# Sorted-block attention and a four-expert layer on one core: the key mix in full-width matmuls, a new order of batch 1's stages, and four smaller edits

## The chip, the cores and the metric

The kernel runs on one core of a Trainium2 chip. The metric is the time of one execution on the device, in microseconds (us). Medians are quoted with their range. A ratio is the mean time of one kernel's fast runs over the mean time of the other kernel's fast runs of the same rounds, so it is not quite the ratio of the medians that stand beside it; its 95% interval is given. The profile shows one execution: for the kernel before a further one of 374.80 us. Its span is some 1.8 us shorter than its time.

Engines are called TensorE (PE in the profile, its weight loads PEld), VectorE (DVE), ScalarE (ACT), GpSimd (POOL) and the sync engine (SP), which only issues transfers.

## The reference, cut to what matters

```python
# q, k, v: (4 batches, 8 heads, 768, 64); 8 blocks of 96 rows; sort_net: (4, 8, 8, 8)
for _ in range(5):                        # Sinkhorn rounds: a soft permutation P of the blocks
    P = exp(P - max(P)); P /= P.sum(-1); P /= P.sum(-2)
k_sorted = einsum('bhij,bhjcd->bhicd', P, k_blocks)     # "mix" of keys; the same for v
attn = softmax(q_blocks @ k_sorted_blocks.T / 8)        # within each block
x = (attn @ v_sorted_blocks)  -> (3072, 512)
# four experts, each x -> 1024 -> 512, weighted by domain_probs
out = sum_e p[:, e] * (relu(x @ w1[e]) @ w2[e])
```

## The kernel before

Batches go through in order. While the experts work on batch b, the attention of batch b+1 is slipped between their matmuls: a plan names, for every slot (after each group of first-layer matmuls and after each of seven second-layer products), the stages to issue. A stage is one of: mix of values (`st_v`), mix of keys (`st_k`), transpose of queries by a transfer (`st_q`), scores (`st_s`), outputs (`st_a`), transpose of outputs by a transfer (`st_x`), or loads. Two heads form a "pair"; a batch has four, and three pairs of row blocks ("row block pair" c = 0, 1, 2) in the expert part.

```python
def st_k(b, pr):                          # 12 matmuls, 64 weight columns each
    ps = psa([P, R, P], F32, ...)         # psa: pool of two buffers; psm: another pool of two
    for r in range(R):                    # R = 6 rows of a partition
        for hh in range(2):
            nc.tensor.matmul(ps[ds(D * hh, D), r, :], head(b, "k", h)[:, r, :], PIk..., ...)
    nc.scalar.copy(kT..., ps...)          # one copy of 128 x 768

PLAN0 = [ ...                             # batch 1, slots of c = 1 and 2, cut
    (1, 0, st_q, 1), (1, 0, st_s, 0), (1, 0, st_n, 2), (1, 1, st_k, 1), (1, 1, st_v, 2), (1, 2, st_v, 3),
    (1, 3, st_a, 0), (1, 4, st_x, 0), (1, 3, st_q, 2), (1, 4, st_n, 3), (1, 5, st_s, 1), (1, 6, st_k, 2),
    (1, 8, st_a, 1), ..., (1, 10, st_s, 2), ..., (1, 11, st_k, 3), (1, 12, st_a, 2), ...,
    (2, 1, st_x, 2), ..., (2, 2, st_s, 3), (2, 8, st_a, 3), (2, 9, st_x, 3) ]

def chunk(b, c, slot, done=()):
    chunk_first(...)                      # first layer; VectorE evacuates each group
    for w in range(1, 4 if b or c else 3):
        h_sums(E - 1, w)                  # sums that the products p5, p6, p7 need
    ...                                   # then products p1, p4, p2, p5, p6, p7, p3
            next(sums0)                   # weight differences for the next batch, on VectorE
            tt(u2[:], product("p6", ...), p1[:], ALU.add)

def store(n, tile):
    nc.sync.dma_start(o[:, 2 * c + n, :], tile[:])
```

The softmax here doesn't subtract the row's maximum and nothing guards it: scores larger than these inputs give would overflow.

## Time and profile before

375.43 us median of 3 runs (375.1 to 376.16).

| part of the page | value |
|---|---|
| span | 373.0 us |
| TensorE busy | 366.3 us, 98% |
| VectorE, ScalarE, GpSimd busy | 261.2, 73.9, 87.9 us |
| chain that ended last | TensorE 87%, transfers 8% |

The chain is followed back from the last instruction, at each step to what released it. The groups of instructions give busy time and mean nanoseconds after the first bar, and idle time ahead of them after the second. Two groups of the kernel before, the key mix and its copy:

```profile
L376 PE MATMUL ps_k<-PIk,nat_k 128*64 128x128 f16 x144 | 6.3, 223 | 0.0
...
L383 ACT CAST kT<-ps_k 128x768 f16<-128x768 f32 x12 | 9.6, 799 | 35.4 <-PE ps_k L376 35.3
```

"128*64" is the array that the weights fill: half of the columns. The mix itself is 6.3 of 366 us.

### The profile page before, as it was taken

Reading aid. Unit: us, or ns where it says so; the run is one execution under the profiler, and the core shown is the slowest. Engines: PE = TensorE matmul, PEld = TensorE weight load, DVE = VectorE, ACT = ScalarE, POOL = GpSimd, SP = SyncE. Lnnn points to the kernel's source line nnn. Section 1 sums busy time; section 2 is a strip of 40 time slices with the busy share of each in tenths; the row PEclk is TensorE's granted clock in tenths of the full one; section 3 lists DMA queues with packets and bytes.
Section 4 is the critical chain, followed back from the end, with each engine's and each line's share of the span. In section 5 each row is a group of like instructions: output and inputs, shape, how many; then the busy total and the mean of one; then the engine's idle time right before and its main releaser. Section 6 shows DMA issues by size and latency. Waiting matters only on the chain.

```text
span 373.0 us, 9188 instructions
## 1 busy us (share of the span) xinstructions
PE 366.3 (98%) x4013; PEld 314.9 (84%) x4013; DVE 261.2 (70%) x470; ACT 73.9 (20%) x120; POOL 87.9 (24%) x122
## 2 busy tenths in 40 slices
PE   8999999999999999999999999999999999999996
PEld 8785858888888888888898888888889888888885
DVE  5654798679888774795694684696695693774872
ACT  2673330423210233012100224012101000000000
POOL 8772101804577203002911000000000001001001
PEclk9999999999999999999999999999999999999999
DMA  7999999999995658642962322505203101121001
GB/s 104 207 207 229 208 209 197 190 163 143 187 154 137 110 77 133 126 80 43 124 71 48 101 66 60 138 2 77 79 2 79 57 15 44 56 47 50 19 3 56
DMA packets 69603, 38.25 MB, mean 103 GB/s; under 512 B 40374, under 2 KB 64444, under 8 KB 69564
## 3 DMA queue, kind: packets, MB, share of 16 engines
q0 software_dynamic: 34640, 17.83, 37.6%
q1 hardware_dynamic: 34924, 19.85, 26.0%
q8 instruction: 31, 0.51, 0.6%
q14 instruction: 8, 0.07, 0.1%
HBM read 42.00 MB, written 6.34 MB: 130 GB/s over the span
## 4 chain that ended last, share of the span: by engine, by line
PE 87%; DMA 8%; DVE 2%; POOL 1%; issue 1%; ACT 0%; DVEq 0%
PE ps_h L730 40%; PE ps_p L763 35%; DMA w<-in_moe_w_dram 4%; PE ps_o L670 3%; DMA qT<-natq 2%; PE ps_w L241 2%; DMA natq<-in_q_dram 2%; PE ps_h L635 1%; PE ps_s L393 1%; PE ps_a L425 1%; PE ps_k L376 1%; PE ps_v L345 1%; POOL sn L284 0%; DVE xsl L410 0%; POOL T L136 0%
## 5 line engine op out<-in xcount | busy, mean ns | idle before, releaser
L730 PE MATMUL ps_h<-xT,w 128*128 128x256 f16 x1440 | 163.0, 273 | 0.0
L730 PEld LDWEIGHTS <-w 128*128 128x128 f16 x1440 | 139.5, 98 | 17.8
L736 DVE SCALAR_TENSOR_TENSOR Hb<-ps_h,pb 128x1024 f16<-128x1024 f32 x90 | 110.1, 1224 | 40.1 <-PE ps_h L730 38.3
L763 PEld LDWEIGHTS <-Sb 128*128 128x128 f16 x720 | 69.5, 98 | 9.6 <-issue 0.5
L763 PEld LDWEIGHTS <-Hb 128*128 128x128 f16 x540 | 52.1, 98 | 6.8 <-issue 0.4
L790 POOL TENSOR_TENSOR oa<-u,p 128x256 f32<-128x256 f32 x9 | 6.5, 723 | 176.7 <-issue 161.9
L763 PE MATMUL ps_p<-w,Sb 128*128 128x256 f16 x360 | 43.2, 273 | 0.3 <-DVE u L863 0.3
L763 PE MATMUL ps_p<-w,Hb 128*128 128x256 f16 x360 | 43.2, 273 | 0.0
L763 PE MATMUL ps_p<-T,Sb 128*128 128x256 f16 x360 | 42.3, 273 | 0.0
L400 ACT ACTIVATE ET<-ps_s 96x768 f16<-96x768 f32 x24 | 18.1, 802 | 54.4 <-PE ps_s L393 54.4
L114 POOL DMA_DIRECT2D natq<-in_q_dram x24 | 19.9, 851 | 14.3 <-DMA w<-in_moe_w_dram 10.2
L778 ACT COPY p<-ps_p 128x256 f32<-128x256 f32 x9 | 3.4, 373 | 93.3 <-PE ps_p L763 50.1
L763 PE MATMUL ps_p<-T,Hb 128*128 128x256 f16 x180 | 21.6, 273 | 0.0
L715 DVE TENSOR_TENSOR Sb<-Sb,Hb 128x512 f16<-128x512 f16 x45 | 19.6, 436 | 0.4
L717 DVE TENSOR_TENSOR Sb<-Hb 128x512 f16<-128x512 f16 x45 | 18.8, 418 | 0.0
L713 DVE TENSOR_TENSOR Sb<-Hb 128x512 f16<-128x512 f16 x45 | 18.8, 417 | 0.0
L410 DVE TENSOR_TENSOR xsl<-ps_a,rz 96x512 f16<-96x512 f32 x24 | 16.5, 686 | 0.8
L719 DVE TENSOR_TENSOR Sb<-Hb,Sb 128x512 f16<-128x512 f16 x45 | 16.6, 427 | 0.0
L383 ACT CAST kT<-ps_k 128x768 f16<-128x768 f32 x12 | 9.6, 799 | 35.4 <-PE ps_k L376 35.3
L788 DVE TENSOR_TENSOR u<-ps_p,p 128x256 f32<-128x256 f32 x9 | 3.8, 426 | 17.9 <-PE ps_p L763 17.9
L351 ACT CAST vo<-ps_v 128x768 f16<-128x768 f32 x12 | 9.5, 801 | 21.5 <-PE ps_v L345 19.8
L103 POOL DMA_DIRECT2D nat_k<-in_k_dram x8 | 6.1, 767 | 31.9 <-PE ps_k L376 27.8
(131 smaller groups left out, 300.9 us busy)
## 6 DMA issues: line engine op xcount, KB each, us to landing
w<-in_moe_w_dram POOLq DMA_DIRECT2D x7, 1024.0 KB, 27.1
pb<-p_dram SPq DMA_DIRECT2D x12, 512.0 KB, 5.1
nat_k<-in_k_dram POOLq DMA_DIRECT2D x8, 384.0 KB, 7.4
nat_v<-in_v_dram POOLq DMA_DIRECT2D x8, 384.0 KB, 8.6
vs<-vo SPq DMA_DIRECT2D x36, 66.0 KB, 4.6
natq<-in_q_dram POOLq DMA_DIRECT2D x24, 96.0 KB, 4.5
out_dram<-ob SPq DMA_DIRECT2D x9, 256.0 KB, 2.3
out_dram<-oa SPq DMA_DIRECT2D x9, 256.0 KB, 2.3
```

Source lines behind the costliest of these rows:

```text
L114: nc.gpsimd.dma_start(t[:, h // 2, :, h % 2, :], q[b, h].rearrange("(t p) d -> p t d", p=P))
L383: nc.scalar.copy(kT[:, 0:S].rearrange("p (i r c) -> p i r c", i=NB, r=R), ps.rearrange("p r (i c) -> p i r c", c=CP),)
L400: nc.scalar.activation(ETs[2 * (pr % 2) + hh][:, 0:S].rearrange("c (a x) -> c a x", a=2), pss[hh][0:BLK, :, 0:HS], AF.Exp, bias=0.0, scale ...
L410: nc.vector.tensor_tensor(xsl[:, :, hh, :].rearrange("c (a i) d -> c a i d", a=2), av[:, :, :, 0:D], rz[:].broadcast_to([BLK, 2, HB, D]), ...
L670: nc.tensor.matmul(ps, h0(fc)[:, ds(t * P, P)], w2sb[0][:, fc, :], start=(fc == 0), stop=(fc == NFC - 1),)
L713: tt(sm[0], blk(0, 1), blk(1, 1), ALU.add)
L715: tt(sm[1], sm[0], blk(0, 0), ALU.subtract)
L717: tt(sm[2], blk(0, 0), blk(0, 1), ALU.subtract)
L719: tt(sm[3], blk(1, 0), sm[1], ALU.subtract)
L730: nc.tensor.matmul(ps[:, f, :], w1sb[e][:, kc, ds((4 * g + f) * P, P)], xT[:, kc, ds(2 * c * P, 2 * P)], start=(kc == 0), stop=(kc == NKC ...
L736: nc.vector.scalar_tensor_tensor(out=Hb[:, e, ds(4 * g, 4), :], in0=ps[:], scalar=0.0, op0=ALU.max, in1=pb[:, ds(e, 1), :].broadcast_to([P ...
L763: nc.tensor.matmul(ps[:], lhs(e, f), Ts[e][rhs][:, f, :], start=(e == es[0] and f == 0), stop=(e == E - 1 and f == KH - 1),)
```

## The change

It has six parts: **keys** (two rows at a time, full-width weights, hence four copies of a quarter each), **plan** (batch 1's outputs later, but for the last pair's; its second scores and its last outputs one slot sooner), **sums** (the last sums and the weight differences later on VectorE, the first product in the other pool), **start** (query transposes in the fifth Sinkhorn round), **copy** (one copy from VectorE to ScalarE) and **store** (the last row block in two parts).

```diff
 def warm(n):
-        ps = psA.tile(...)
+        ps = psM.tile(...)
 for it in range(5):
-        if it >= 3:
-            h_q(it - 3, 0, nc.scalar.copy)
-            warm(20 - 8 * (it - 3))
+        if it == 4:
+            for qd in range(2):
+                h_q(qd, 0, nc.scalar.copy)
+            warm(30)
 def st_k(b, pr):
-        ps = psa([P, R, P], F32, ...)
-        for r in range(R):
-            for hh in range(2):
-                nc.tensor.matmul(ps[ds(D * hh, D), r, :], head(b, "k", h)[:, r, :], PIk..., ...)
-        nc.scalar.copy(kT..., ps...)
+        ps = psa([P, 2, 512], F32, ...)
+        for hh in range(2):
+            for a in range(R // 2):
+                nc.tensor.matmul(pk[:, hh, a, :],
+                    head(b, "k", h)[:, ds(2 * a, 2), :].rearrange("p r d -> p (r d)"), PIk..., ...)
+        for hh in range(2):
+            for r in range(2):
+                nc.scalar.copy(kT[ds(D * hh, D), r], pk[ds(D * r, D), hh]...)
 PLAN0 (slots of c = 1 and 2, cut)
-        (1, 3, st_a, 0), (1, 4, st_x, 0), (1, 5, st_s, 1), (1, 6, st_k, 2), (1, 8, st_a, 1),
-        (1, 10, st_s, 2), (1, 11, st_k, 3), (1, 12, st_a, 2), (2, 2, st_s, 3), (2, 8, st_a, 3), (2, 9, st_x, 3),
+        (1, 4, st_s, 1), (1, 5, st_a, 0), (1, 6, st_x, 0), (1, 7, st_k, 2), (1, 9, st_a, 1),
+        (1, 11, st_s, 2), (2, 0, st_a, 2), (2, 1, st_k, 3), (2, 3, st_s, 3), (2, 7, st_a, 3), (2, 8, st_x, 3),
 chunk
-        for w in range(1, 4 if b or c else 3):
+        for w in range(1, 4 if b else 2 if c else 3):
             h_sums(E - 1, w)
+            parts = 2 if (b, c) == (B - 1, R // 2 - 1) else 1
+            if parts == 2:
+                nc.sync.dma_start(o[:, 2 * c, 0:DH], oa1)      # right after p2
 ...                                                            # and oa2 alone at the end
-            nc.scalar.copy(p1[:], product("p1", ..., "b11"))
+            nc.scalar.copy(p1[:], product("p1", ..., "b11", psm if c == 1 else psa))
+            if c == 1: h_sums(E - 1, 2); h_sums(E - 1, 3)      # after p4
             f2()
+            if c == 2: h_sums(E - 1, 2); h_sums(E - 1, 3)      # after p2
-            next(sums0)
             tt(u2[:], product("p6", ...), p1[:], ALU.add)
+            next(sums0)                                        # the second one likewise after u3
-        [(h_w, 1, vec), (h_a, 0, 2)],
+        [(h_w, 1, act), (h_a, 0, 2)],
```

More of the change, by code (lines that the diff above doesn't have):

```diff
@@ L237, in warm @@
     def warm(n):
-        ps = psA.tile([P, 4, P], F32, tag="ps", name=f"ps_w_{state['n']}")
+        ps = psM.tile([P, 4, P], F32, tag="ps", name=f"ps_w_{state['n']}")
         state["n"] += 1
@@ L371, in st_k @@
     def st_k(b, pr):
-        ps = psa([P, R, P], F32, f"ps_k_{b}_{pr}")
-        for r in range(R):
-            for hh in range(2):
-                h = 2 * pr + hh
+        ps = psa([P, 2, 512], F32, f"ps_k_{b}_{pr}")
+        pk = ps[:, :, 0:R // 2 * P].rearrange("p h (a x) -> p h a x", x=P)
+        for hh in range(2):
+            h = 2 * pr + hh
+            for a in range(R // 2):
                 nc.tensor.matmul(
-                    ps[ds(D * hh, D), r, :],
-                    head(b, "k", h)[:, r, :],
+                    pk[:, hh, a, :],
+                    head(b, "k", h)[:, ds(2 * a, 2), :].rearrange("p r d -> p (r d)"),
                     PIk[(b * H + h) // 4][:, h % 4, :, :].rearrange("p i c -> p (i c)"),
@@ L381, in st_k @@
                 )
-        kT = kTs[pr % 2]
-        nc.scalar.copy(
-            kT[:, 0:S].rearrange("p (i r c) -> p i r c", i=NB, r=R),
-            ps.rearrange("p r (i c) -> p i r c", c=CP),
-        )
+        kT = kTs[pr % 2][:, 0:S].rearrange("p (i a r c) -> p r a i c", a=R // 2, r=2, c=CP)
+        for hh in range(2):
+            for r in range(2):
+                nc.scalar.copy(
+                    kT[ds(D * hh, D), r],
+                    pk[ds(D * r, D), hh].rearrange("p a (i c) -> p a i c", c=CP),
+                )
     def st_s(b, pr):
@@ L601 @@
         (0, 9, st_v, 0), (0, 10, st_q, 0), (0, 10, st_v, 1), (0, 11, st_k, 0), (0, 11, st_n, 1), (1, 0, st_q, 1),
-        (1, 0, st_s, 0), (1, 0, st_n, 2), (1, 1, st_k, 1), (1, 1, st_v, 2), (1, 2, st_v, 3), (1, 3, st_a, 0),
-        (1, 4, st_x, 0), (1, 3, st_q, 2), (1, 4, st_n, 3), (1, 5, st_s, 1), (1, 6, st_k, 2), (1, 8, st_a, 1),
-        (1, 7, st_lv, 0), (1, 9, st_x, 1), (1, 10, st_s, 2), (1, 9, st_lv, 1), (1, 9, st_q, 3), (1, 11, st_k, 3),
-        (1, 12, st_a, 2), (1, 12, st_lk, 0),
-        (2, 0, st_lq, 0), (2, 1, st_x, 2), (2, 2, st_lk, 1), (2, 2, st_s, 3), (2, 8, st_a, 3), (2, 9, st_x, 3),
+        (1, 0, st_s, 0), (1, 0, st_n, 2), (1, 1, st_k, 1), (1, 1, st_v, 2), (1, 2, st_v, 3), (1, 3, st_q, 2),
+        (1, 4, st_s, 1), (1, 4, st_n, 3), (1, 5, st_a, 0), (1, 6, st_x, 0), (1, 7, st_k, 2), (1, 7, st_lv, 0),
+        (1, 9, st_a, 1), (1, 9, st_q, 3), (1, 9, st_lv, 1), (1, 10, st_x, 1), (1, 11, st_s, 2), (1, 12, st_lk, 0),
+        (2, 0, st_a, 2), (2, 0, st_lq, 0), (2, 1, st_k, 3), (2, 2, st_x, 2), (2, 2, st_lk, 1), (2, 3, st_s, 3),
+        (2, 7, st_a, 3), (2, 8, st_x, 3),
     ]
@@ L757, in chunk, with product @@
         sm = lambda n: (lambda e, f: Sb[:, n, e, ds(f * P, P)])
-        def product(n, lhs, rhs):
-            ps = psm([P, DH], F32, f"ps_{n}_{b}_{c}")
+        def product(n, lhs, rhs, pool=psm):
+            ps = pool([P, DH], F32, f"ps_{n}_{b}_{c}")
             for e in es:
@@ L797, in chunk @@
             slot()
-            nc.sync.dma_start(o[:, 2 * c, :], oa[:])
+            if parts == 2:
+                nc.sync.dma_start(o[:, 2 * c, DH:Dm], oa2)
+            else:
+                nc.sync.dma_start(o[:, 2 * c, :], oa[:])
             return
         def f1():
-            nc.scalar.copy(p1[:], product("p1", blk(0, 0), "b11"))
+            nc.scalar.copy(p1[:], product("p1", blk(0, 0), "b11", psm if c == 1 else psa))
             slot()
@@ L857, in chunk @@
             f4()
-            f2()
+            if c == 1:
+                h_sums(E - 1, 2)
+                h_sums(E - 1, 3)
+            f2()
+            if c == 2:
+                h_sums(E - 1, 2)
+                h_sums(E - 1, 3)
             f5()
@@ L861, in chunk @@
                 h_sums(e, 4)
-            next(sums0)
             tt(u2[:], product("p6", sm(1), "t2"), p1[:], ALU.add)
             slot()
+            next(sums0)
             gtt(oa2, u2[:], oa2, ALU.add)
-            next(sums0)
             tt(u3[:], product("p7", sm(2), "t3"), u2[:], ALU.add)
@@ L869, in chunk @@
             last(u3[:])
+            next(sums0)
             store(1, ob)
```

## The prediction

> **What bounds the kernel now.** I read the page's busy shares first, then its two chain lines, then the merged chain in order of time, and last the timeline of TensorE where that chain leaves it. From the page:
>
> ```profile
> PE 366.3 (98%) x4013; PEld 314.9 (84%) x4013; DVE 261.2 (70%) x470; ACT 73.9 (20%) x120; POOL 87.9 (24%) x122
> ...
> PE 87%; DMA 8%; DVE 2%; POOL 1%; issue 1%; ACT 0%; DVEq 0%
> ```
>
> TensorE is busy 98% of the span and makes 87% of the chain that ended last; the DMA's 8% is the part to place. The table by stretches gives TensorE 172.00 of 172.00 us busy between 118 and 290 us, and 79.00 of 79.00 between 290 and 369. "Busy" alone proves little, so I check the rate: 16 matmuls of 128x256 take 1.75 us (109 ns each), everywhere in those stretches. From 118 us on only fewer or cheaper matmuls, or a shorter end, can save time. Before 118 us the chain leaves TensorE at the places shown here (start, duration, what):
>
> ```profile
> 14.29 14.12 DMA w<-in_moe_w_dram
> ...
> 69.25 7.02 DMA natq<-in_q_dram
> 76.27 0.02 issue
> 76.29 7.88 DMA qT<-natq
> 84.17 0.14 issue
> 84.30 0.52 PE ps_s L393 x16
> ```
>
> The first second-layer weight lands at 28.41 us and TensorE begins with it at 28.46. The queries of batch 1's second head pair land at 76.27, their transpose is issued at 76.29 and lands at 84.17, and that pair's scores begin at 84.30. On the timeline of TensorE these scores waited only 0.32 us: they reached their place almost exactly when the data came. One more wait, 0.31 us, follows 32 us later:
>
> ```profile
> 84.30 0.52 PE L393 MATMUL ps_s<-qT,kT 64*128 64x96 f16 x16 [0.32 <-DMA qT<-natq]
> ...
> 116.61 1.47 PE L763 MATMUL ps_p<-w,Sb 128*128 128x256 f16 x12 [0.31 <-DVE u L863]
> ```
>
> **What the Trainium skill says.** TensorEngine Tiling (Array Packing), "Key Properties", says that a change of tiling mode drains the TensorE, and its "Restrictions" that column tiling disables the fast weight load. The trace agrees with a cost at the change of mode. In the chain, a mix of keys (64 weight columns) and a mix of values (128) stand between the same first-layer matmuls:
>
> ```profile
> 123.64 0.33 PE ps_v L345 x2
> 123.97 1.75 PE ps_h L730 x16
> 125.72 0.46 PE ps_k L376 x12
> 126.17 5.35 PE ps_h L730 x48
> ```
>
> After the values 16 matmuls take 1.75 us; after the keys 48 take 5.35, which is 0.11 more than 48 x 0.109 = 5.24. Every key mix leaves this 0.11, and so does every score group (also a partial array); no value or output group does. TensorE: Matmul & The Clock Gate, "Back-to-back issue gap", gives 134 cycles for a warm isolated 128-column matmul, some 56 ns at the 2.4 GHz it states; the trace agrees, with 8 full transposes of 128 columns in 0.45 us (35.53 to 35.99), 56 ns each. ScalarE: Activation LUTs, "What ACT_TABLE_LOAD costs", gives a fixed part plus a part per element of a lane, whatever the partitions; the trace agrees: a copy of 384 elements takes 477 ns and one of 768 takes 799, so four quarter copies cost more than one. DMA: Bandwidth & Descriptors, "HWDGE ordering", says each DMA engine consumes one row's descriptors in ring order; that is why the transpose of 76.29 stands behind two output stores issued at 72.96.
>
> **The change part by part.**
>
> Keys. 144 matmuls with 64 weight columns become 72 with 128; twelve mixes in all, 12 matmuls each before and 6 after. One mix now costs 0.455 us and leaves 0.107 us behind it, 0.562 together. Afterwards 6 x 56 ns = 0.336 us and, as for the values, nothing behind. Saved: 0.226 us per mix, 2.7 us over twelve, all of it TensorE time. The price is on ScalarE: one copy of 799 ns becomes four of at most 477 ns, 1.9 us, so 12 x 1.1 = 13 us more on an engine that is busy 74 of 373. The scores come two or three groups of 1.75 us after their keys, and I find about half a microsecond left in the tightest place (keys, a copy of p5, a value copy, then scores: 1.9 + 0.4 + 0.8 us against 4.2). So hidden.
>
> Deferred sums. The 0.31 us at 116.3 comes from VectorE: three sums and one weight difference of 1.2 us stand before the evacuation that frees TensorE's buffer. The change puts the weight difference after that evacuation and spreads sums 2 and 3 over earlier gaps. Saved 0.31, perhaps with 0.1 given back at another place, because VectorE has almost no idle time there (29.86 of 34.00 us busy between 84 and 118).
>
> Plan of batch 1. Now the order of TensorE after the value mixes is: outputs of pair 0 (0.48), two groups (3.5), scores of pair 1. The changed order, read from the built kernel, is: two groups, scores of pair 1, one group (1.75), outputs of pair 0 (0.48). The scores are thus asked for 1.75 + 0.48 = 2.2 us sooner. With two key mixes made shorter (0.45), TensorE arrives at 84.0 - 2.2 - 0.45 = 81.3 us. The transpose is not sooner: the loads of queries queue behind the weights and the natural keys in one software queue that moves some 200 GB/s without a break from 4 us on (slices of the page), and this change moves none of those issues. So TensorE waits about 3 us instead of 0.3, and what it saved before 84 us is spent in that wait. The later output stages move back by one to four slots, and the last transposed output is asked for one slot sooner, before the next batch's first group; I expect no new wait there.
>
> Start. Both query transposes go into the fifth Sinkhorn round, behind its exponential; the 0.80 us copy that stood before it (9.29 to 10.09) no longer delays the chain, worth up to 0.5 us, and a copy moved to ScalarE takes away a wait of 0.23 us at 37.5. Both lie before 84 us: the first runs into the weight that lands at 28.41, the second into the wait for the queries. Worth nothing.
>
> End. Today:
>
> ```profile
> 367.37 1.91 PE L763 MATMUL ps_p<-w,Sb 128*128 128x256 f16 x16
> ...
> 369.39 0.42 DVE L796 TENSOR_TENSOR oa<-ps_p,oa 128x256 f32<-128x256 f32 x1 [0.25 <-PE ps_p L763]
> 369.84 0.33 SPq L798 DMA_DIRECT2D out_dram<-oa  x1
> ```
>
> The last store of 256 KB lands 2.05 us after its issue. Half of it can go earlier. At the 207 GB/s of the page's fullest early slices 256 KB are 1.3 us, so half is at most 0.6; but the other row block's store, issued at 369.20, still shares the engines, and the half row makes smaller packets. I take a third of it as my estimate, 0.2 us.
>
> **The sum.** Counted from the scores at 84.30 us, which I hold to stay where they are: the group and the outputs now behind them +2.23; ten remaining key mixes -2.26; the wait at 116.3 -0.31; the end -0.2. Together -0.5 us: 375.43 becomes 374.9. I lean a little lower, to 374.6, for the case that the transpose comes sooner.
>
> **The rivals.** (a) The transpose is not fixed. If it lands as early as TensorE asks (81.3 us), the whole saving of 2.7 + 0.3 + 0.3 + 0.2 shows, and the time is about 372. For it: it lands 7.9 us after its issue, though a typical one takes 4.9, so crowding matters. Against it: the crowd (four query loads issued 71.4 to 74.8, two stores, six value moves) is the same after the change. (b) The four copies on ScalarE become a wait: scores wait for keys, or a value mix waits for a buffer of the pool of two. For it: half a microsecond of room in each of two batches, and next to none at the value mix of batch 1. If the estimate of 1.9 us is short by a microsecond, each of eight mixes could cost some tenths: 376. Against it: three of the four mixes of a batch have slots to spare. (c) VectorE becomes the bound between 84 and 118 us, where outputs now meet other evacuations: up to 1 us, 375.9. Against it: it catches up during the wait for the queries. (d) A wait of 3 us lets the granted clock fall; the row of the page shows 9s throughout now, so nothing measured speaks for it.
>
> **Range and chances.** The case of the sum has three chances in four, with half a microsecond to either side; rival (a), whole or in part, one in five, 372 to 374; (b) to (d) the rest. Hence 372.6 to 375.9. Faster by 2% needs 367.9, more than all parts together; slower by 2% needs 382.9, for which no part has the size.
>
> **What would show it.** Keys: 72 matmuls near 56 ns, the group behind each mix back at 1.75 us, ScalarE busy about 87 us. Plan: a wait of 2 to 3 us on the queries' transpose before batch 1's second score group, landing near 84 us; if it is under 1 us, my step about the fixed landing is wrong and the time nearer 372. Sums: no wait at the last product of the second row block pair. End: last store landing under 2 us. New waits of scores on ScalarE, or of products on VectorE in batch 1, would make the prediction too low.

## The result, and the profile after

| set | before | changed | ratio, 95% interval |
|---|---|---|---|
| first | 375.26 (375.0 to 376.16), 4 runs | 372.96 (372.77 to 373.35), 4 runs | 0.9936, 0.9917 to 0.9955 |
| repeat 1, another chip | 375.81 (374.36 to 377.51), 11 runs | 374.21 (372.78 to 375.95), 6 runs | 0.9961, 0.9930 to 0.9992 |
| repeat 2, another chip | 375.00 (373.99 to 375.91), 11 runs | 374.64 (372.93 to 375.44), 6 runs | 0.9981, 0.9958 to 1.0004 |

The change is faster by 0.2 to 0.6%, inside the range that the prediction gave (372.6 to 375.9) and within 2%. The first set is the kindest of the three; in the third the interval reaches 1, so that this set alone does not show a gain. From the page of the changed kernel (span 371.0 us), busy shares and chain:

```profile
PE 362.8 (98%) x3939; PEld 314.8 (85%) x3939; DVE 259.9 (70%) x469; ACT 87.8 (24%) x157; POOL 86.0 (23%) x122
...
PE 85%; DMA 7%; DVE 4%; ACT 2%; POOL 1%; issue 1%; DVEq 0%; ACTq 0%
```

TensorE lost 3.5 us of busy time, ScalarE gained 13.9 (13 were predicted; the copies of the keys went from 9.6 to 22.7). The groups of the key mix and its copy, and the mix in the merged chain of batch 2 (start, duration, what):

```profile
L379 PE MATMUL ps_k<-PIk,nat_k 128*128 128x128 f16 x72 | 6.0, 219 | 0.2 <-DVE xsl L415 0.2
...
L388 ACT CAST kT<-ps_k 64x384 f16<-64x384 f32 x48 | 22.7, 473 | 37.9 <-PE ps_k L379 37.0
```

```profile
125.87 0.34 PE ps_k L379 x6
126.20 5.24 PE ps_h L735 x48
```

The mix went from 0.46 to 0.34 us and the 48 matmuls behind it from 5.35 to 5.24, as the prediction had it. (The 6.0 us of the group is no contradiction: "busy" counts the modelled end of each matmul, which overlaps the next instruction; the distance from start to start is what tells.) Now the waits of TensorE in batch 1: the chain to the second scores, and three places of the timeline.

```profile
68.92 6.63 DMA natq<-in_q_dram
75.56 7.31 DMA qT<-natq
82.92 0.51 PE ps_s L398 x16
```

```profile
82.92 0.51 PE L398 MATMUL ps_s<-qT,kT 64*128 64x96 f16 x16 [1.81 <-DMA qT<-natq]
...
100.53 0.51 PE L379 MATMUL ps_k<-PIk,nat_k 128*128 128x128 f16 x6 [0.23 <-DVE xsl L415]
...
116.76 1.47 PE L769 MATMUL ps_p<-w,Sb 128*128 128x256 f16 x12
```

TensorE came to the scores of pair 1 at 81.1 us and waited 1.81 us for the transposed queries; the wait at 116.6 is gone, and a new one of 0.23 us stands at the last keys. Cut at these scores, at the first group of batch 1's expert part (its first matmul) and at the start of the last matmul, the two traces compare so (read from the traces, us):

| stretch | before | changed | difference | predicted |
|---|---|---|---|---|
| start to the scores of pair 1 | 84.30 | 82.92 | -1.38 | 0 |
| scores of pair 1 to batch 1's first group | 33.62 | 35.15 | +1.53 | +1.47 |
| from there to the last matmul | 251.09 | 249.27 | -1.82 | -1.81 |
| last matmul to the end | 4.00 | 3.66 | -0.34 | -0.2 |
| span | 373.0 | 371.0 | -2.0 | -0.5 |

The predicted +1.47 is 2.23 for the moved group and outputs, less two key mixes (0.45) and the wait of 0.31. The last three stretches came out near what was worked, the second only with the new wait of 0.23 us in it: a trace without that wait (start undone, below) has 34.84 there, +1.22. The first stretch did not come out. The experiments are about that stretch, about what the plan is worth, and about why the repeats are slower than the first set.

### The profile page after: what moved, and what is told of

Its sections match the earlier page's. It is cut to its first block, busy times and chain, and to the rows that moved or that the text cites. A ratio compares the mean times of both kernels' runs of the same rounds, so it can differ in the third digit from the quotient of the medians.

```text
span 371.0 us, 9075 instructions
## 1 busy us (share of the span) xinstructions
PE 362.8 (98%) x3939; PEld 314.8 (85%) x3939; DVE 259.9 (70%) x469; ACT 87.8 (24%) x157; POOL 86.0 (23%) x122
## 4 chain that ended last, share of the span: by engine, by line
PE 85%; DMA 7%; DVE 4%; ACT 2%; POOL 1%; issue 1%; DVEq 0%; ACTq 0%
PE ps_h L735 39%; PE ps_p L769 33%; PE ps_h L640 3%; DMA xT<-xsl 3%; PE ps_o L675 3%; DMA qT<-natq 2%; DMA natq<-in_q_dram 2%; PE ps_s L398 1%; PE ps_a L430 1%; PE ps_k L379 1%; PE ps_v L346 1%; PE ps_mk L467 1%; DVE xsl L415 1%; PE ps_s L522 1%; DMA sn<-in_sort_net_dram 0%
## 5 line engine op out<-in xcount | busy, mean ns | idle before, releaser
L388 ACT CAST kT<-ps_k 64x384 f16<-64x384 f32 x48 | 22.7, 473 | 37.9 <-PE ps_k L379 37.0
L720 DVE TENSOR_TENSOR Sb<-Sb,Hb 128x512 f16<-128x512 f16 x45 | 18.8, 418 | 0.4
L415 DVE TENSOR_TENSOR xsl<-ps_a,rz 96x512 f16<-96x512 f32 x24 | 16.5, 687 | 1.1 <-DMA xT<-xsl 0.3
```

The source lines that it names most:

```text
L388: nc.scalar.copy(kT[ds(D * hh, D), r], pk[ds(D * r, D), hh].rearrange("p a (i c) -> p a i c", c=CP),)
L415: nc.vector.tensor_tensor(xsl[:, :, hh, :].rearrange("c (a i) d -> c a i d", a=2), av[:, :, :, 0:D], rz[:].broadcast_to([BLK, 2, HB, D]), ...
L720: tt(sm[1], sm[0], blk(0, 0), ALU.subtract)
```

## The experiments

Twelve runs were made of ten kernels (two of them the changed kernel, one the kernel before, one version twice), in three sets, each on one chip. All gave the correct result. Because the arrival of loads scatters, I read stretches within a trace beside the times.

**Undo the plan** (the changed kernel with the old plan of batch 1):

```diff
-PLAN0 = [new order]
+PLAN0 = [order of the kernel before]
```

> The changed kernel with the old plan of batch 1; keys, sums, start and store stay changed. My theory: the new plan asks for the scores of pair 1 by 2.2 us too soon, and the wait of 1.81 us before them is its price. With the old plan TensorE comes to them at 81.1 + 2.2 = 83.3 us, after the landing at 82.9, so the wait goes and the time falls by about 1.8 us, to 371.2 (up to 371.7 if VectorE's evacuations, which the new plan spreads, hold TensorE by some tenths). Rival: the new plan pays for itself elsewhere, by keeping VectorE out of TensorE's way between 84 and 118 us; then the time is 373.0 or more, with new waits on VectorE.

Measured: 373.58 us (372.45 to 376.56) against 375.07 before, ratio 0.9959 (0.9927 to 0.9991). No gain of 1.8 us shows. TensorE's waits in its timeline:

```profile
85.93 1.47 PE L769 MATMUL ps_p<-w,Hb 128*128 128x256 f16 x12 [0.36 <-DVE Hb L741]
...
97.76 0.40 PE L430 MATMUL ps_a<-vs,ET 96*128 96x65 f16 x8 [0.55 <-ACT kT L388]
...
117.92 1.47 PE L769 MATMUL ps_p<-w,Sb 128*128 128x256 f16 x12 [0.28 <-DVE u L881]
```

The scores of pair 1 waited for nothing, as I expected, but three other waits came, 1.2 us together. The middle one is the price of the keys: the old plan puts the outputs of pair 2 one product after the keys of pair 3, and they wait for a buffer until the four copies are done. From the first group of the second row block pair to batch 1's first group it took 47.24 us here and 47.54 in the changed kernel's first trace. So the rival was nearer the truth: the new plan has one long wait in place of three short ones, and in these two traces the two are about level as long as the clock holds (see below). The changed kernel did not run on this chip, so the times do not compare them.

**Undo the start:**

```diff
-        if it == 4: both query transposes, warm(30)
+        if it >= 3: one query transpose, warm(20 or 12)
```

> The changed kernel with the old start (one query transpose in each of the last two Sinkhorn rounds). The transposed queries landed 1.3 us sooner in the changed kernel than I held to be possible. Theory A: the start's lead of 0.43 us at the issue of the loads (13.86 against 14.29) passes down the full software queue to the transpose; then here the transpose lands at 83.3 to 84.2, the wait grows to 2.2 to 3.1 us, and the time is 373.4 to 374.2. Theory B (my prediction): the queue is bound by its rate and the lead is lost; then the landing stays near 82.9 within its scatter from run to run and the time at 373.0.

Measured: 374.22 us (373.19 to 375.36), ratio 0.9968 (0.9942 to 0.9994). In its trace TensorE began with the first second-layer weight at 28.31 us, against 28.32, 28.50 and 28.20 in three traces of the changed kernel, and the transpose landed at 83.54, against 82.87, 83.49 and 83.37. By the letter this is what theory A forecast (landing 83.3 to 84.2, a wait of 2.33 us, 374.2 us). But the changed kernel itself, traced twice more, landed at nearly the same time, so theory A is not needed: the start buys nothing that can be seen, as predicted. A lead under a few tenths in the landing can't be excluded from one trace.

**Undo the keys:**

```diff
-        6 matmuls of 128 weight columns, 4 copies
+        12 matmuls of 64 weight columns, 1 copy
```

> The changed kernel with the old mix of keys (twelve matmuls of 64 weight columns). Theory: a mix costs 0.226 us more of TensorE's time; ten mixes stand after the wait for the queries, so 2.26 us more, while the two before it only shorten the wait, from 1.8 to about 1.35 us: 375.2. Rival: the four copies on ScalarE give part of it back through later scores; then undoing costs less, 374.5 or under, and the changed kernel's waits for kT on ScalarE shrink here.

Measured: 376.61 us (375.52 to 378.01), ratio 1.0034 (1.0010 to 1.0058): slower than the kernel before. In the trace, from batch 1's first group to the last matmul it takes 251.09 us, to the hundredth what it takes in the kernel before; with the new keys it is 249.27, 249.28 and 249.28 in the three traces of the changed kernel. Eight mixes stand there, so 1.82 / 8 = 0.227 us each. The chip of this set had no run of the changed kernel, so of the time I only say that undoing the keys takes away all of the gain and more. It is above the 375.2 that I expected; four of the six executions have a lowered clock, and the other two took 375.52 and 376.19. The wait at the scores of pair 1 was 1.69 us. In the stretch after batch 1's first group no part of the 1.82 us is given back by ScalarE.

```profile
127.46 0.53 PE L377 MATMUL ps_k<-PIk,nat_k 128*64 128x128 f16 x12
127.92 5.42 PE L731 MATMUL ps_h<-xT,w 128*128 128x256 f16 x48
```

(On the timeline a duration runs to the modelled end; from start to start the old mix takes 0.46.)

**The plan alone, on the kernel before:**

```diff
-PLAN0 = [order of the kernel before]
+PLAN0 = [new order]
```

> The kernel before with the new plan of batch 1 alone. Theory: with the old keys TensorE comes to the scores of pair 1 at 84.0 - 2.2 = 81.8 us and waits for the transpose, which lands near 84.2: a wait of 2.4 us against 0.3, while nothing else is gained but the small waits on VectorE: 0.5 to 1.5 us slower than the kernel before. Rival: the plan is what made the changed kernel faster; then this is faster than the kernel before by over 0.3 us.

Measured: 377.43 us (376.51 to 379.75), ratio 1.0059 (1.0025 to 1.0093), so 0.6% slower. The wait at the scores of pair 1 was only 0.86 us in this trace, because an earlier wait (1.45 us at the scores of pair 0, for their own queries) had already made TensorE late; the rest of the loss lies between the scores and batch 1's first group, 36.32 us against 33.62. Its timeline also shows where the sums matter:

```profile
83.86 0.51 PE L393 MATMUL ps_s<-qT,kT 64*128 64x96 f16 x16 [0.86 <-DMA qT<-natq]
...
96.84 1.47 PE L763 MATMUL ps_p<-w,Sb 128*128 128x256 f16 x12 [0.48 <-DVE u L863]
```

**Undo the sums:**

```diff
-        sums 2 and 3 after p4 or p2; weight differences after the evacuations of p6 and p7
+        sums 1 to 3 ahead of p1; weight differences ahead of those evacuations; p1 always in psm
```

> The changed kernel with the old order of the last sums, of the weight differences and of the buffer of the first product. Theory of my prediction: the 0.31 us wait at the last product of the third row block pair comes back (0.2 to 0.5 us), and perhaps one more of that size after the second pair: 0.3 to 0.6 us slower than the changed kernel. Rival: the new plan alone had removed it, by having the last output group one slot sooner; then no such wait shows and the time is within 0.1 us.

Measured: 375.75 us (374.08 to 376.62), ratio 0.9986 (0.9954 to 1.0017), against 0.9961 for the changed kernel in the same set; the intervals overlap, so the times do not tell what the sums are worth. The timeline:

```profile
93.13 1.47 PE L768 MATMUL ps_p<-w,Sb 128*128 128x256 f16 x12 [0.31 <-DVE oacc L826]
...
98.63 1.47 PE L768 MATMUL ps_p<-w,Sb 128*128 128x256 f16 x12 [0.48 <-DVE u L875]
```

Two waits, 0.79 us, both in the *second* row block pair; none in the third, where I had expected the old 0.31 back. Put beside the others it is clear: the wait at the third pair is there in both kernels with the old plan (0.31 before, 0.28 with the plan undone, sums deferred or not) and in neither with the new plan and the old sums. So the plan alone is enough to remove it. What the deferred sums remove are two waits in the second pair that the new plan would otherwise have (here 0.31 and 0.48, with the plan alone 0.48).

**The changed kernel again**, twice, for its own scatter:

> The changed kernel again, on the chip of this set, so that the others can be read against it, and a second trace of it. The traces so far show the second-layer weight landing anywhere from 27.9 to 29.8 us in kernels with the same start, and with it everything up to the scores of pair 1 is moved. If that scatter belongs to the loads and not to the change, this trace will show the landing of pair 1's transposed queries away from 82.9 us by up to 1.5 us, the wait at its scores between 1.4 and 2.4 us, and from the first group of batch 1 to the end of TensorE again 249.3 us. Time 372.8 to 373.6.

> The changed kernel once more, as the measure of this set. In its repeat before, the wait of 2.24 us at the scores of pair 1 was followed by some 6 us at a granted clock of 0.7 to 0.9, which cost 1.3 us; of that set's six executions two had a clock of 0.991 to 0.994 over the span and took 374.8 and 376.0 us. Theory: the long wait brings the clock down in a part of the executions, so here too the executions under 0.996 are longer by 1.5 to 2 us than those at 1.0, which take 372.8 to 374. Rival: the clock falls by chance whatever the wait; then the kernels without the long wait in this set fall as often.

Measured: 374.21 us (372.78 to 375.95) and 374.64 us (372.93 to 375.44); the ratios are in the table above. The transpose landed at 83.49 and 83.37, and TensorE waited 2.24 and 1.97 us. But the stretch from the scores to batch 1's first group took 36.47 and 36.48 us instead of 35.15, without any wait in it. The reason, from the timeline of the first repeat and from its table by stretches (the third number from the end is PEclk, the granted share of the clock):

```profile
83.54 0.52 PE L398 MATMUL ps_s<-qT,kT 64*128 64x96 f16 x16 [2.24 <-DMA qT<-natq]
83.98 2.73 PE L735 MATMUL ps_h<-xT,w 128*128 128x256 f16 x16
```

```profile
83.00:84.00 1.00, 0.46 (x17) 0.39 (x18) 0.00 (x0) 0.00 (x0) 0.00 (x0) 1.00 1.21 107
84.00:85.00 1.00, 1.00 (x13) 0.88 (x10) 0.00 (x0) 0.92 (x2) 0.00 (x0) 0.97 1.21 115
85.00:86.00 1.00, 1.00 (x7) 0.74 (x5) 0.00 (x0) 0.59 (x1) 0.00 (x0) 0.50 1.36 110
...
88.00:89.00 1.00, 1.00 (x10) 0.84 (x8) 0.97 (x4) 0.00 (x0) 0.00 (x0) 0.83 0.00 0
```

From shortly before 85 to shortly after 88 us the clock is at half, and a group of 16 that took 1.92 us takes 2.73. The cost is 36.47 - 34.84 = 1.6 us, read against the trace with the start undone, which has neither a dip nor a wait in that stretch (the 35.15 hold the wait of 0.23 us). The dip lasts 3.4 us; half of that, 1.7 us, is lost to TensorE.

Of the fourteen traces six hold such a dip, each 3.4 us long (summed from the clock in steps of 0.1 us). In five of them TensorE had waited long just before: 2.24 and 1.97 us here, 2.34 with the sums undone, 4.83 and 3.40 in the two attempts below. The dip begins 2.8 to 4.1 us after the start of the wait, in the two attempts while TensorE still stands. With the sums undone:

```profile
84.04 0.52 PE L398 MATMUL ps_s<-qT,kT 64*128 64x96 f16 x16 [2.34 <-DMA qT<-natq]
84.49 3.53 PE L735 MATMUL ps_h<-xT,w 128*128 128x256 f16 x16
```

Five traces with waits of 1.29 to 1.81 us after 70 us have no dip there. There are two exceptions. A wait of 2.33 us (start undone) was not followed by a dip. And the trace with the keys undone has its dip at 16.5 to 20 us, long before the new plan acts and with no wait above 0.72 us in the 15 us before it; its own 1.69 us at the scores brought none.

The executions without a trace give only the mean clock, and one dip makes that about 0.995 wherever it lies. At or under 0.995 are 6 of 16 executions of the changed kernel and 2 of 33 of the kernel before. On the two chips of the repeats the changed kernel's six executions at 0.998 and above average 373.4 us and the six at 0.995 and under 375.1. Kernels with the new plan and another part undone fall as often (start 4 of 6, sums 4 of 6, keys 4 of 6; the plan alone 3 of 6), those without the wait seldom (plan undone 1 of 6, stores moved 1 of 6 in each of two sets). The first set had none in four, which fits its looking best. So a wait of some 2 us or more goes with the dip in most traces, but not in all, and it is not the only thing that brings one; what decides is not shown. The expectation above speaks of some 6 us at 0.7 to 0.9: that was read from a coarser table. Its forecast that the slow executions are 1.5 to 2 us longer came true (1.9 in the second repeat); the 372.8 to 373.6 us forecast for the first repeat did not.

**Move the two stores behind the query transpose:**

```diff
 def store(n, tile):
-        nc.sync.dma_start(o[:, 2 * c + n, :], tile[:])
+        if (b, c) == (0, 0): held.append((o[:, 2 * c + n, :], tile[:]))
+        else: nc.sync.dma_start(o[:, 2 * c + n, :], tile[:])
 # st_q, after its transpose is issued
+        while held: nc.sync.dma_start(*held.pop(0))
```

> The changed kernel with the two output stores of the first row block pair (512 KB) issued behind the query transpose of pair 1 instead of ahead of it, in the same queue. Theory: the transpose's 7.3 us from issue to landing are its place behind those stores, which land at 79.5 and 80.5 us; with them behind it, it lands at 79 to 81.5 us, the wait at the scores shrinks from 1.8 us to under 0.5, and the time falls to 371.2 to 371.7. Rival: the crowd of small query loads of the software queue, which lasts until 81.9 us, holds it as much; then it lands after 82 us and the time stays above 372.3.

> The changed kernel with the two stores behind the query transpose, against the changed kernel on the same chip. Theory: no wait at the scores of pair 1 (landing near 81.4 us), 0.5 to 0.9 us at the last keys instead, hence 0.8 to 1.3 us faster than the changed kernel, and a lowered clock in at most one or two of six executions. Rival: the crowd of transfers behind it makes up for it and it is within 0.4 us of the changed kernel.

Measured: 372.83 us (371.71 to 374.96), ratio 0.9943 (0.9913 to 0.9973), on one chip, and 373.88 us (372.35 to 377.35), ratio 0.9987 (0.9949 to 1.0025), on another, where the changed kernel had 0.9981. The transpose took 5.50 and 5.31 us from issue to landing instead of 7.3 to 7.9, and the wait at the scores is gone. The times forecast, 371.2 to 371.7 and 0.8 to 1.3 us under the changed kernel, were not reached. The lines (first trace, issues of the sync engine, then TensorE and VectorE):

```profile
75.95 1.23 SPq L368 DMA_TRANSPOSE qT<-natq  x1
77.28 1.00 SPq L372 DMA_DIRECT2D out_dram<-oacc  x2
```

```profile
81.49 0.52 PE L401 MATMUL ps_s<-qT,kT 64*128 64x96 f16 x16
...
99.66 0.51 PE L382 MATMUL ps_k<-PIk,nat_k 128*128 128x128 f16 x6 [0.79 <-DVE xsl L418]
```

```profile
98.92 0.69 DVE L418 TENSOR_TENSOR xsl<-ps_a,rz 96x512 f16<-96x512 f32 x1 [0.91 <-DMA xT<-xsl]
```

So the landing was not fixed: its place in the queue was worth some 2 us. But most of that comes back as 0.8 to 1.0 us at the last keys: VectorE can't write new outputs until an earlier one, issued for transpose at 87.49 and landed at 98.82, has left its buffer. The times don't tell this version from the changed kernel on the one chip where both ran; whether it is better stays open.

**Two attempts at that next wait**, both on top of the moved stores: the last keys ahead of the outputs of pair 2, and a third buffer for the outputs (paid for by one buffer less for the transposed queries).

```diff
 # keys ahead
-        (2, 0, st_a, 2), (2, 0, st_lq, 0), (2, 1, st_k, 3), (2, 2, st_x, 2)
+        (2, 0, st_k, 3), (2, 0, st_lq, 0), (2, 1, st_a, 2), (2, 2, st_x, 2)
 # third buffer
-        xsl = att.tile(..., tag="xsl")            qT = att.tile(..., tag="qT", bufs=3)
+        xsl = att.tile(..., tag="xsl", bufs=3)    qT = att.tile(..., tag="qT", bufs=2)
```

> The changed kernel with the two stores behind the query transpose, and with the last keys of batch 1 before the outputs of pair 2 instead of after them. In the trace with the stores alone moved there was no wait at the scores of pair 1, but one of 0.79 us at those last keys: they waited for a buffer that VectorE held, which itself waited 0.91 us for a transposed output to leave. If that is all, both waits are gone here, and the time lies 1.3 to 2.0 us under the changed kernel's, near 371.3. Rival: the transfers between 88 and 100 us are so crowded that the next stage waits in their place; then it is within 0.7 us of the kernel with the stores alone moved, and another wait of some tenths shows between 95 and 118 us.

> The same with a third buffer for the normalized outputs, paid for by one buffer less for the transposed queries. Theory: the 0.79 us wait at the last keys comes from VectorE waiting for the first transposed output to leave its buffer; with a third buffer it is gone, and the time falls by another 0.4 to 0.8 us, near 371.8. Rival: TensorE only comes sooner to the first group of batch 1 and waits there for the last transposed output, which landed 0.8 us ahead of need; then the gain is under 0.2 us, and if that transpose is late the wait can be several us, as in the version with the keys moved.

Measured: 377.43 us (374.23 to 378.93), ratio 1.0034 (0.9996 to 1.0072), and 377.04 us (376.40 to 379.36), ratio 1.0061 (1.0038 to 1.0085). Both are 2 to 3 us slower than the changed kernel of their set (374.21 and 374.64). Neither theory came true; the rival of the second did, with a wait of several us for the last transposed output. The wait at the last keys is gone in both, and TensorE reached batch 1's first group at 117.0 and 117.9 us; there it stood, in the timelines of the first and the second:

```profile
121.83 4.63 PE L738 MATMUL ps_h<-xT,w 128*128 128x256 f16 x29 [4.83 <-DMA xT<-xsl]
```

```profile
121.32 4.69 PE L738 MATMUL ps_h<-xT,w 128*128 128x256 f16 x29 [3.40 <-DMA xT<-xsl]
```

The last transposed output lands at 121.3 to 121.8 us, 2 to 4 us later than in three traces of the changed kernel (117.67 to 119.26), though it was issued sooner: it took 10.0 and 8.6 us to land instead of 3.8 to 4.3. All six executions of each have a lowered clock. So in these two versions a transfer, not TensorE's speed, sets when batch 1 can begin. Why it is so late was not tested. The traces show that the eight loads of the next queries were issued from 102.6 and 103.3 us on instead of 100.3 (stores moved, first trace), and that a load of keys landed at 121.3 and 120.7, just ahead of that output, instead of 114.4.

**The kernel before, a second trace:**

> The kernel before, for a second trace: is the landing of 84.17 us usual? In seven traces of other versions with the stores ahead of the transpose it lay between 82.9 and 84.6. I expect 83 to 84.7 here, the scores of pair 1 between 84.0 and 84.8 whichever it is, since TensorE comes there at 84.0 at the soonest, and a time of 374.4 to 377.

Measured: 376.19 us, one run. The transpose landed at 83.68, yet the scores of pair 1 began at 84.18, with no wait: TensorE came no sooner. And 1.29 us were lost at batch 1's first group, on the same last transposed output:

```profile
84.18 0.52 PE L393 MATMUL ps_s<-qT,kT 64*128 64x96 f16 x16
...
119.64 1.58 PE L730 MATMUL ps_h<-xT,w 128*128 128x256 f16 x13 [1.29 <-DMA xT<-xsl]
```

## Why the prediction was right or wrong, point by point

- **Keys: right, to the hundredth.** 0.226 us per mix was worked out from 0.455 + 0.107 - 0.336; 0.227 was measured: 249.27 to 249.28 us in six traces with the new keys and no wait in that stretch, 251.09 or 251.10 in three with the old. By the starts of the matmuls the loss lies at both ends of the mix: 202 ns from the last first-layer matmul to the mix's first instead of 109, and 151 ns from its last to the next full-width one instead of 55, with 120 instead of 109 once after it. Inside, the pairs start 56 ns apart, as the full-width ones do, but for the first step of some 80. So the prediction's 0.107 behind the mix is there (96 + 11 ns), while most of what it counted as the mix itself, 0.119, lies ahead of it (93 ns). Of the fast weight load, which it names too, the traces show only that a load of 64 columns takes 109 ns and one of 128 takes 98. That the copies stay hidden was right for this plan. The tightest place was not the one I named but in batch 1 under the old plan, where it cost 0.55 us; the new plan had moved it out of the way.
- **Plan: right in kind, short in size.** The wait at the scores came, 1.81 to 2.24 us instead of the 3 of the working. I called it a loss paid by nothing. Alone it is one (0.6% slower); together with the keys it takes away three waits of 1.2 us, which I had not seen. (The outputs moved by one or two slots, not by up to four.)
- **The landing: the step that failed.** The sum was "counted from the scores at 84.30 us, which I hold to stay where they are". They moved to 82.92, 83.54 and 83.42. The one landing of 84.17 in the trace at hand was at the late end (82.9 to 84.6 in ten traces with the stores ahead), and TensorE of the kernel before could not have used a sooner one, since it comes there at 84.0; the changed kernel, there at 81.1, takes all of it. That is 0.8 to 1.4 us, the greater part of what the prediction was short by in the first set. Rival (a) had described this and named its cause (crowding); moving the stores showed that 2 us of the landing were their place in the queue. In the first trace 0.73 of the 1.30 us by which the transpose landed sooner is its sooner issue (the queries' load landed at 75.55 instead of 76.27), and 0.57 its shorter way (7.31 us instead of 7.88); why the load came sooner is not shown. The reason given for a fixed landing, one software queue at some 200 GB/s, was misread from a row that counts all queues: it holds from 4 to 65 us (11.78 MB of some 12.5), but from 65 to 84 the software queue moved 1.21 of 3.34 MB and the hardware queue 2.10.
- **Clock: wrong.** Rival (d) was put aside with "nothing measured speaks for it". After waits of about 2 us the clock did fall to half for 3.4 us in two of three traces of the changed kernel, at 1.6 us each, and the mean clock speaks for such a dip in 6 of 16 executions. This error and that of the landing have opposite signs. In the two traces of the repeats they partly cancel, so that their medians (374.21, 374.64) lie next to the predicted 374.6 by luck, not because the sum was exact.
- **Sums: wrong place.** 0.31 us at the third pair (the prediction's last part calls it the second) was taken away by the plan; the sums save 0.48 to 0.79 in the second pair, in the new plan alone.
- **Start and copy: right.** Worth nothing that the runs can show (the copy was not tried alone).
- **Store: right, a little small.** The stretch after the last matmul is 4.00, 3.99 and 3.98 us in three kernels or traces with one part and 3.63 to 3.66 in eleven traces with two: 0.35 instead of 0.2.
- **Range.** Half a microsecond to either side of the main case was too narrow for a kernel whose executions differ by 3 us; the first set's 372.96 lies below it, and the wider range held only because of the rivals.

## What to carry to other kernels

Count the cost of narrow-weight matmuls with the drains ahead of and behind them: here the two ends were nearly all of the 0.227 us per group, and the matmuls between them kept the pace of the full-width ones. Before a stage is moved earlier on the engine that binds, find the transfer that it needs and ask whether that can come earlier as well; one trace's landing time is a sample, and the kernel before may hide how early it could be. A wait of 2 us on TensorE was followed in most traces by a lowered clock that cost another 1.6 us, so it is worth asking whether one long wait can be broken up into short ones; that this pays was not shown here.

## What the Trainium skill lacked or had wrong

- TensorEngine Tiling (Array Packing), "Key Properties", says that a change of tiling mode drains the TensorE but gives no figure: here a group of half-width matmuls between full-width ones costs 0.227 us more than the same work at full width, by the starts of the matmuls 0.093 us of it ahead of the group and 0.107 behind.
- TensorE: Matmul & The Clock Gate, "Why this matters for your kernels", advises no idle gaps above about 3 us. Here waits of 1.97, 2.24 and 2.34 us were followed by half clock (0.50) for 3.4 us, and waits of 1.81 and 2.33 us were not; one dip came with no wait above 0.72 us in the 15 us before it. For a lone busy core "What's actually happening" on that page knows two states of the clock, full and half; the 0.50 agrees.
- DMA: Bandwidth & Descriptors, "HWDGE ordering", has the ring order; no page gives a time for what it does to a query transpose behind two stores of 256 KB: 7.3 to 7.9 us to landing with the stores ahead of it, 5.1 to 5.5 with them behind.
- ScalarE: Activation LUTs, "What ACT_TABLE_LOAD costs": 186 ns + 0.833 ns per element gives 506 ns for 384 elements and 826 for 768; measured 473 and 799 ns for these copies, which the profile calls CAST (the page's formula is for ACTIVATE with immediate scale and bias; the exponential of 768 elements took 802).
